# Hand-over from a dense block to routed experts: another place for tile 0's output, a later third routing, other row buffers and eight fact buffers

## The chip, the cores and the metric

The kernel runs on one core of one Trainium2 chip. The metric is the time of one execution on the device in microseconds (us), from the first to the last instruction with what lies around them. A profiled execution gives a trace beside its time. The engines are named as in the profile: PE multiplies matrices, PEld loads PE's weights, ACT (ScalarE) and DVE (VectorE) work element by element, POOL (GpSimd) does small operations and issues indirect DMAs, and SP (SyncE) issues the other DMAs; SPq is SP's queue of them.

## The reference, cut to what matters

```python
x = attention(q, k, v, alpha)            # 3072 tokens of 384
h = x @ w_in; x = (h * sigmoid(h)) @ w_out   # dense block, 384 -> 2048 -> 384
logits = normed(x) @ normed(expert_emb).T / tau
e = argmax(logits); gate = softmax(logits)[e]
for each expert e:                       # 8 experts
    out[mask_e] = gate * (relu(x[mask_e] @ w1[e]) @ w2[e])   # 384 -> 1024 -> 384
```

## The kernel before, in words

Tokens go through in blocks of 384, eight in all. The attention of later chunks runs among the dense products of earlier blocks. After a block, `route` is called three times, once for 128 tokens: it squares the row for its norm (L1199), takes the logits and the best expert (L1201 to L1212), counts each token's place in its expert with two small matmuls (L1216, L1217, into `pr`), puts the row in two half-precision words (L1234, L1235), works out its position (L1245) and scatters it with an indirect DMA on POOL (L1248) into `xs_d`, a list in DRAM sorted by expert. A row of 394 words is 384 of data and 10 of facts (token, scale, logits).

After that the expert tiles run, 128 rows of the list each. Tile j has these steps:

- `prep_load(j)`: SP loads the tile's data with a transposing DMA into `xT` (L1440) and its facts into `mt` (L1441). Eight early tiles (0 to 7) have a list of their own, `idx0`, made before the last block ends. For the others `tile_list` makes `idx` on DVE (L1332 to L1399), in words of `g3`, after the last routing.
- `expert1(j, 0)` and `expert1(j, 1)`: 9 matmuls each (L1495) into `hp2`, relu into two half-precision parts on ACT (L1501) and DVE (L1502), in the scratch tile `work`. `send(j, i)` lets SP turn that half with a transposing DMA (L1468): halves of even tiles into `hb` and into `g3[:, 0:1024]`, those of odd tiles into `work`.
- `expert2(j)`: 24 matmuls (L1523) into `po`, the first 12 from the first turned half and the others from the second; ACT scales `po` into `ob` (L1531) and POOL scatters `ob` to the output (L1534).

The last block's three routings (`last(0)`, `last(1)`, `last(2)`) are written among the steps of tiles 0 to 3. POOL also writes rows of padding behind each expert's list, eight DMAs from DRAM to DRAM (L1409). Up to shortly before the hand-over, SP also loads the experts' second weights in pieces (L736); ACT and DVE, or ACT and POOL, split each piece into two half-precision words (L691 and L692, or L560, L563 and L564). The last of these pieces share ACT and DVE with tile 0's relu.

Three things set the order around the change. Each engine and each queue takes its instructions in the order that the built program gives it. This order comes from a scheduler, which goes by the order of the code and its own reckoning. A tile of a pool with `bufs=3` takes one of three places, and waits until its reader before has ended. The row pool (tag "row", three buffers, below A, B and C) holds `xT`, the rows of `route`, and before the change tile 0's `ob`. Tag "sq" is one further buffer; `last(0)`'s row and the later `ob` take turns in it. Before the change buffer A holds tile 0's `xT`, then `last(1)`'s row, then tile 4's `xT`; B holds tile 1's `xT`, tile 0's `ob`, then `last(2)`'s row; C holds the `xT` of tiles 2, 3 and 5.

Of the kernel before, what the change touches and what calls it, by code (L numbers as in the profile page):

```python
# [9 lines left out]
FP32 = mybir.dt.float32  # L10
# [263 lines left out]
def attention_silu_moe_kernel(  # L274
# [57 lines left out]
    NT, DM = out.shape  # L332
# [19 lines left out]
    ROW = DM + E + 2  # L352
# [12 lines left out]
    def guard(kind, thr=0.0, op=ALU.is_lt):  # L365
        if kind not in guards:
            width = {"decay": 2 * NCH, "nat": NCH, "finite": 160}.get(kind, 8)
            t = const.tile([128, width], FP32, name=f"guard_{kind}")
            nc.vector.memset(t, 2.0 * thr if op == ALU.is_lt else 0.0)
            guards[kind] = [t, 0, thr, op]  # L370
        g = guards[kind]
        g[1] += 1
        return g[0][:, g[1] - 1:g[1]]
# [39 lines left out]
    if True:  # L413
# [4 lines left out]
        m2 = wst.enter_context(tc.tile_pool(name="m2", bufs=2, side="right"))  # L418
# [12 lines left out]
        def bank(dims, dtype, name):  # L431
            at = (ps_a, "at")
            wide = [at, at, at, (ps_o, "o0"), (ps_o, "o1"), (ps_o, "o2"), (ps_h, "h"), (ps_h, "h")]
            pool, tag = at if turn[0] is None else wide[turn[0] % 8]
            if turn[0] is not None:
                turn[0] += 1
            return pool.tile(dims, dtype, tag=tag, name=name)
# [12 lines left out]
        g3 = m2.tile([128, 4 * BLK], FP16, name="g3", bufs=1)  # L450
# [966 lines left out]
        def parts(j):  # L1417
            if j < KEARLY:
                return [(slice(0, 128), idx0[0:1, j:j + 1], ei0[0:1, j:j + 1])]
            if j < NFULL:  # L1420
                n = j - KEARLY
                return [(slice(0, 128), idx[0:1, n:n + 1], ei[0:1, n:n + 1])]
            cols = [2 * (j - NFULL) + h for h in range(2)]
            return [
                (slice(64 * h, 64 * h + 64), idx[0:1, NLIST + e:NLIST + e + 1], e) for h, e in enumerate(cols)
            ]

        def prep_load(j):
            d = tl_[j] = {"s": (j - NFULL + SFULL if j >= NFULL else j) % 2}
            d["x"] = xT = m2.tile([128, 2 * KD, 128], FP16, tag="row", name="xT", bufs=3)  # L1430
            mt = m2.tile([128, ROW - DM], FP32, tag="mt", name="mt", bufs=6)
            loads = []
            for ts, src, _ in parts(j):
                r = nc.values_load(
                    src, engines=sp, min_val=0, max_val=DUMMY,
                    skip_runtime_bounds_check_because="a tile starts inside an expert's rows or at the dummy rows",
                )
                size = ts.stop - ts.start
                loads += [
                    nc.sync.dma_start_transpose(out=xT[:, :, ts], in_=xs_d.bitcast(FP16)[bass.ds(r, size), 0:2 * DM]),  # L1440
                    nc.sync.dma_start(out=mt[ts], in_=xs_d[bass.ds(r, size), DM:]),  # L1441
                ]
            if j < KEARLY:
                for ins in loads:
                    for other in scattered[NCH - TPB:] + pads:
                        tc.declare_no_dep(ins.ins, other.ins, reason="early tiles hold tokens of earlier blocks only")
                early_loads.extend(loads)
            d["m"] = mt
# [17 lines left out]
        def send(j, i):  # L1466
            d = tl_[j]
            lead["send"] = nc.sync.dma_start_transpose(  # L1468
                out=d["hT"][i].rearrange("p (c t) -> p c t", t=128), in_=d["hs"][i].rearrange("p s f -> p (s f)")
            )  # L1470

        def expert1(j, i, keep=False):
            d = tl_[j]
            if i == 0:
                d["e"] = [
                    (ts, src if isinstance(src, int) else nc.values_load(
                        src, engines=[mybir.EngineType.PE], min_val=0, max_val=E - 1,
                        skip_runtime_bounds_check_because="the chip clamps the index to an expert",
                    )) for ts, _, src in parts(j)
                ]  # L1480
                s = d["s"]
                d["hs"] = [
                    work[:, 512 * at:512 * (at + 1)].bitcast(FP16).rearrange("p (s f) -> p s f", s=2)
                    for at in ((3, 2) if s else (5, 4))
                ]
                odd = work[:, 0:1024].bitcast(FP16)
                d["hT"] = (odd[:, 0:1024], odd[:, 1024:2048]) if s else (hb, g3[:, 0:1024])
            xT = d["x"]
            fs = slice(i * 512, (i + 1) * 512)
            hp = ps_h.tile([128, 512], FP32, tag="h", name="hp2")  # L1490
            n = 0
            for c in range(KD):
                for a, w in ((c, "h"), (KD + c, "h"), (c, "l")):
                    for ts, e in d["e"]:
                        nc.tensor.matmul(  # L1495
                            out=hp[ts], lhsT=xT[:, a, ts], rhs=w1s[w][c][:, e if isinstance(e, int) else bass.ds(e, 1), fs],
                            start=(n == 0), stop=(n == 3 * KD - 1),
                        )
                    n += 1
            hs = d["hs"][i]  # L1500
            lead["a"] = nc.scalar.activation(out=hs[:, 0], in_=hp, func=ACTF.Relu)  # L1501
            lead["g"] = nc.vector.scalar_tensor_tensor(  # L1502
                out=hs[:, 1], in0=hp, scalar=0.0, in1=hs[:, 0], op0=ALU.max, op1=ALU.subtract
            )
            if not keep:
                send(j, i)

        def expert2(j, part=None):
            d = tl_[j] if part == 0 else tl_.pop(j)
            hT = d["hT"]  # L1510
            if part != 1:
                d["o"] = (
                    bank([128, 512], FP32, "po") if j < 2 else ps_o.tile([128, 512], FP32, tag=f"o{d['s']}", name="po")
                )[:, 0:DM]
            po = d["o"]
            order = [[0, 1, 2, 3], [4, 5, 6, 7]] if part is None else [[[0, 1, 2, 3], [4, 6]], [[5, 7]]][part]
            n, total = (3 * 6 if part == 1 else 0), 3 * KE
            for group in order:
                for a, w in ((0, "h"), (0, "l"), (4, "h")):
                    for c in group:  # L1520
                        at = (a + c % 4) * 128
                        for ts, e in d["e"]:
                            nc.tensor.matmul(  # L1523
                                out=po[ts], lhsT=hT[c // 4][:, at + ts.start:at + ts.stop],
                                rhs=w2s[w][c][:, e if isinstance(e, int) else bass.ds(e, 1), :], start=(n == 0), stop=(n == total - 1),
                            )
                        n += 1
            if part == 0:
                return
            ob = m2.tile([128, ROW], FP32, name="ob", **(dict(tag="sq", bufs=1) if j else dict(tag="row", bufs=3)))[:, 0:DM]  # L1530
            nc.scalar.activation(  # L1531
                out=ob, in_=po, func=ACTF.Copy, scale=d["fac"], accum_out=guard("finite", 0.0, ALU.not_equal)
            )
            lead["o"] = nc.gpsimd.indirect_dma_start(  # L1534
                out=out[:, :], out_offset=bass.IndirectOffsetOnAxis(ap=d["row"], axis=0),
                in_=ob, in_offset=None, bounds_check=NT - 1, oob_is_err=False,
            )
# [26 lines left out]
        def block(j):  # L1564
# [3 lines left out]
            if last:  # L1568
                early()
                prep_load(0)  # L1570
                prep_load(1)
                prep_load(2)
# [45 lines left out]
        last = lambda t: route(NCH - TPB + t, acc[t])  # L1618
# [14 lines left out]
        expert1(1, 1)  # L1633
        assert not todo and not late
        expert2(0, 0)
        last(0)
        last(1)
        expert1(2, 0, True)
        expert1(2, 1, True)
        expert2(0, 1)  # L1640
        send(2, 0)
        send(2, 1)
        prep_load(3)
        last(2)
        expert2(1)
        expert1(3, 0)
        expert1(3, 1)
        prep_load(4)
        tile_list()
        order = [*range(SFULL), *range(NFULL, NFULL + SPAIR)]  # L1650
        for n in range(2, len(order)):
            j = order[n]
# [68 lines left out]
```

## Time and profile before

| | us |
|---|---|
| median of three runs | 779.56 (778.83 to 782.80) |
| the profiled execution's own time | 775.31 |
| its span, first to last instruction | 773.7 |
| PE busy in the span | 735.0 (95%) |
| DVE, ACT, POOL busy | 499.1, 414.4, 235.7 |
| mean granted TensorE clock | 0.988 of full |

A busy share is a mean over stages with different limits: the attention and dense stages up to about 535 us, the hand-over from 535 to 580 us, the expert tiles from there. A row of the timeline reads: start, duration, engine, line, operation, what it writes and reads, and in brackets how long the engine had been idle and what ended that. For SPq and POOL DMA rows the duration is that of issuing; when the data lands is not in it.

### The profile page before, as it was taken

The page shows a single profiled execution, that of the slowest core. Times are in us where ns is not written, and L with a number is a line of the kernel's source. Part 1 is how long each engine was busy: PE and PEld are TensorE (multiplying, and loading weights), DVE is VectorE, ACT ScalarE, POOL GpSimd, SP SyncE. Part 2 cuts the span into 40 slices and gives each one's busy share as a digit, 9 for nine tenths or more (in the row PEclk, how much of TensorE's full clock was granted, in tenths as well). Part 3 has the DMA queues.
Part 4 walks back from the last instruction along what each step waited for, and adds up shares of the span by engine and source line. Part 5 has one row for each costly group of instructions (what it writes and reads, how often), then busy time and mean ns, then how long its engine had stood idle before and what let it go on. Part 6 is the DMA issues. An engine that isn't in the chain of part 4 may idle for free. (4 is left out here: it accounts for less than half of the span.)

```text
span 773.7 us, 16578 instructions
## 1 busy us (share of the span) xinstructions
PE 735.0 (95%) x5577; PEld 459.5 (59%) x5577; DVE 499.1 (64%) x1434; ACT 414.4 (54%) x936; POOL 235.7 (30%) x328
## 2 busy tenths in 40 slices
PE   8878989999999999999999999999959999999995
PEld 6746655666676667666666655555425555555553
DVE  7999878677897978887877684766632222121221
ACT  4655556567576766856767675767412222222221
POOL 3404235434453653543243020402222111111111
PEclk9999999999999999999999999999989999999998
DMA  9998453435465555464422464267687666756661
GB/s 208 229 318 224 85 91 56 108 65 100 110 127 134 109 130 116 93 151 93 89 88 71 152 189 142 63 177 237 111 165 142 118 128 122 123 103 120 119 107 40
DMA packets 248204, 99.64 MB, mean 129 GB/s; under 512 B 229145, under 2 KB 237502, under 8 KB 247984
## 3 DMA queue, kind: packets, MB, share of 16 engines
q1 hardware_dynamic: 244528, 87.29, 52.5%
q0 software_dynamic: 3584, 11.18, 4.2%
q8 instruction: 51, 0.84, 0.5%
q14 instruction: 41, 0.34, 0.1%
HBM read 58.39 MB, written 12.16 MB: 91 GB/s over the span
## 5 line engine op out<-in xcount | busy, mean ns | idle before, releaser
L1171 PE MATMUL o<-wo_h,w2l 128*128 128x392 f16 x528 | 145.7, 330 | 2.3 <-DVE w2l L1157 1.7
L1502 DVE SCALAR_TENSOR_TENSOR work<-hp,work 128x512 f16<-128x512 f32 x56 | 38.7, 690 | 145.4 <-ACT work L1501 145.4
L1148 PE MATMUL hp<-w2l,wi_h 128*128 128x384 f16 x480 | 118.7, 326 | 0.3 <-ACT w2l L1155 0.3
L1495 PE MATMUL hp<-w1h,xT 128*128 (+1 forms) x384 | 101.1, 382 | 8.3 <-DMA xT<-xs_d 8.1
L1171 PEld LDWEIGHTS <-w2l 128*128 128x128 f16 x792 | 75.3, 98 | 52.9 <-DVE w2l L1157 4.1
L1148 PEld LDWEIGHTS <-wi_h 128*128 128x128 f16 x768 | 74.6, 98 | 49.6 <-issue 3.0
L1495 PEld LDWEIGHTS <-xT 128*128 128x128 f16 (+1 forms) x576 | 50.5, 101 | 65.5 <-DMA xT<-xs_d 7.9
L1171 PE MATMUL o<-wo_l,w2l 128*128 128x392 f16 x264 | 87.4, 331 | 0.0
L1534 POOL DMA_INDIRECT out_dram<-ob,mt x28 | 27.8, 994 | 175.3 <-ACT ob L1531 167.0
L1148 PE MATMUL hp<-w2l,wi_l 128*128 128x384 f16 x240 | 78.2, 326 | 0.0
L1148 PE MATMUL hp<-w2h,wi_h 128*128 128x384 f16 x288 | 71.4, 329 | 1.4 <-ACT w2l L1155 1.0
L1501 ACT ACTIVATE work<-hp 128x512 f16<-128x512 f32 x56 | 33.3, 596 | 72.7 <-PE hp L1495 71.6
L1157 DVE SCALAR_TENSOR_TENSOR w2l<-w2l 128x384 f16<-128x384 f32 x88 | 54.1, 617 | 22.7 <-ACT w2l L1156 22.5
L1171 PE MATMUL o<-wo_h,g 128*128 128x392 f16 x240 | 67.1, 331 | 1.0 <-DVE g L1157 0.7
L1155 ACT ACTIVATE w2l<-hp 128x384 f32<-128x384 f32 x88 | 42.6, 486 | 40.5 <-PE hp L1148 37.8
L1495 PE MATMUL hp<-w1l,xT 128*128 (+1 forms) x192 | 64.3, 382 | 0.0
L1531 ACT ACTIVATE ob<-po,s 128x384 f32<-128x384 f32 x28 | 16.3, 582 | 82.2 <-PE po L1523 75.9
L895 POOL TENSOR_SCALAR_AFFINE_SELECT S<-S 128x512 f32<-128x512 f32 x48 | 32.9, 710 | 85.4 <-ACT S L894 85.3
L1148 PEld LDWEIGHTS <-wi_l 128*128 128x128 f16 x384 | 37.5, 98 | 26.8 <-DVE wi_l L602 2.6
L1171 PEld LDWEIGHTS <-g 128*128 128x128 f16 x360 | 34.9, 99 | 24.6 <-issue 1.3
L1148 PE MATMUL hp<-w2h,wi_l 128*128 128x384 f16 x144 | 46.2, 326 | 1.7 <-DVE wi_l L602 1.7
L1156 ACT ACTIVATE w2l<-w2l 128x384 f16<-128x384 f32 x88 | 45.7, 524 | 2.3 <-PE o L1171 0.4
(299 smaller groups left out, 1546.6 us busy)
## 6 DMA issues: line engine op xcount, KB each, us to landing
work<-in_moe_w_dram SPq DMA_DIRECT2D x24, 512.0 KB, 3.6
work<-in_moe_w_dram SPq DMA_DIRECT2D x30, 384.0 KB, 3.5
nat_a<-in_alpha_dram SPq DMA_DIRECT2D x23, 192.0 KB, 3.2
nat_k<-in_k_dram SPq DMA_DIRECT2D x23, 192.0 KB, 3.1
nat_q<-in_q_dram SPq DMA_DIRECT2D x23, 192.0 KB, 3.2
nat_v<-in_v_dram SPq DMA_DIRECT2D x23, 192.0 KB, 3.0
w1h<-in_moe_w_in_dram SPq DMA_DIRECT2D x5, 768.0 KB, 6.1
w1h<-in_moe_w_out_dram SPq DMA_DIRECT2D x5, 768.0 KB, 7.5
```

Of the source, the lines that this page charges most:

```text
L895: nc.gpsimd.affine_select(out=s, in_=s, pattern=[[0, NPAIR], [1, 128]], compare_op=ALU.is_ge, fill=0.0, base=0, channel_multiplier=-1,)
L1148: ins = nc.tensor.matmul(out=hp, lhsT=wi[a][f // 2][:, c, (f % 2) * 128:(f % 2 + 1) * 128], rhs=x[:, c, :], start=(n == 0), stop=(n == 3 * ...
L1155: nc.scalar.activation(out=g, in_=hp, func=ACTF.Silu, scale=1.0 / (SX * SWI))
L1156: lead["a"] = nc.scalar.activation(out=gh, in_=g, func=ACTF.Copy, scale=SG)
L1157: lead["g"] = nc.vector.scalar_tensor_tensor(out=gl, in0=g, scalar=SG, in1=gh, op0=ALU.mult, op1=ALU.subtract)
L1171: nc.tensor.matmul(out=acc[t], lhsT=a[:, ts], rhs=wo[w][f // 2][:, f % 2, :], start=(f == 0 and n == 0), stop=(f == KF - 1 and n == 2),)
L1495: nc.tensor.matmul(out=hp[ts], lhsT=xT[:, a, ts], rhs=w1s[w][c][:, e if isinstance(e, int) else bass.ds(e, 1), fs], start=(n == 0), stop=( ...
L1501: lead["a"] = nc.scalar.activation(out=hs[:, 0], in_=hp, func=ACTF.Relu)
L1502: lead["g"] = nc.vector.scalar_tensor_tensor(out=hs[:, 1], in0=hp, scalar=0.0, in1=hs[:, 0], op0=ALU.max, op1=ALU.subtract)
L1531: nc.scalar.activation(out=ob, in_=po, func=ACTF.Copy, scale=d["fac"], accum_out=guard("finite", 0.0, ALU.not_equal))
L1534: lead["o"] = nc.gpsimd.indirect_dma_start(out=out[:, :], out_offset=bass.IndirectOffsetOnAxis(ap=d["row"], axis=0), in_=ob, in_offset=Non ...
```

## The change

Tile 0's `ob` goes into the last 768 half-precision words of `g3`, read as 384 words of 32 bits. Of these the first 256 lie in tile 0's second turned half, which its 24 matmuls have read by then. The loads of tiles 3 and 4 are written before tile 2's second half is sent, and `last(2)` after tile 3's two halves. There are eight `mt` buffers in place of six.

```diff
         def prep_load(j):
             d = tl_[j] = {"s": (j - NFULL + SFULL if j >= NFULL else j) % 2}
             d["x"] = xT = m2.tile([128, 2 * KD, 128], FP16, tag="row", name="xT", bufs=3)
-            mt = m2.tile([128, ROW - DM], FP32, tag="mt", name="mt", bufs=6)
+            mt = m2.tile([128, ROW - DM], FP32, tag="mt", name="mt", bufs=8)
...
-            ob = m2.tile([128, ROW], FP32, name="ob", **(dict(tag="sq", bufs=1) if j else dict(tag="row", bufs=3)))[:, 0:DM]
+            ob = m2.tile([128, ROW], FP32, tag="sq", name="ob", bufs=1)[:, 0:DM] if j else g3[:, 2 * DM:].bitcast(FP32)
...
         expert2(0, 1)
         send(2, 0)
+        prep_load(3)
+        prep_load(4)
         send(2, 1)
-        prep_load(3)
-        last(2)
         expert2(1)
         expert1(3, 0)
         expert1(3, 1)
-        prep_load(4)
+        last(2)
         tile_list()
```

By the addresses in the built program, buffer B now holds tile 1's `xT`, then tile 3's, then `last(2)`'s row; C holds tile 2's `xT`, then tile 4's, then tile 6's; A holds tile 0's, then `last(1)`'s row, then tile 5's `xT`.

The scheduler moves more than the code does. On SP, among the last pieces of the experts' weights, three loads of facts (of tiles 3, 4 and 5) stood before and there are now five. The first two of them have not moved; this is the place of the third, before the change:

```order
L736 DMA work_109<-in_moe2_w2_dram 128x2x384
L1434 TENSOR_LOAD idx0_209
L1441 ISA
L1441 DMA mt_7766<-xs_d_60 128x10
L736 DMA work_109<-in_moe2_w2_dram 128x2x384 x5
```

and with it (the last three rows of facts are those of tiles 5, 6 and 7):

```order
L736 DMA work_109<-in_moe2_w2_dram 128x2x384
L1434 TENSOR_LOAD idx0_209
L1441 ISA
L1441 DMA mt_7765<-xs_d_60 128x10
L1434 TENSOR_LOAD idx0_209
L1441 ISA
L1441 DMA mt_7816<-xs_d_60 128x10
L1434 TENSOR_LOAD idx0_209
L1441 ISA
L1441 DMA mt_7896<-xs_d_60 128x10
L736 DMA work_109<-in_moe2_w2_dram 128x2x384 x5
```

The facts of tiles 6 and 7 stood behind the hand-over's transposes before; now two more reads of the list and two more loads stand ahead of the next five pieces of weights.

Further on, SP at the hand-over, before (`g3` and `hb` are halves of even tiles, `work` from `work` of odd ones; xT_7615, 7716 and 7765 are tiles 3, 4 and 5):

```order
L1468 DMA_TRANSPOSE g3_179<-work_109 128x8x128
L1468 DMA_TRANSPOSE work_109<-work_109 128x8x128 x2
L1468 DMA_TRANSPOSE hb_7404<-work_109 128x8x128
...
L1440 DMA_TRANSPOSE xT_7615<-xs_d_60 128x6x128
...
L1441 DMA mt_7817<-xs_d_60 128x10
L1468 DMA_TRANSPOSE g3_179<-work_109 128x8x128
...
L1441 DMA mt_7897<-xs_d_60 128x10
...
L1440 DMA_TRANSPOSE xT_7716<-xs_d_60 128x6x128
L1468 DMA_TRANSPOSE work_109<-work_109 128x8x128 x2
...
L1440 DMA_TRANSPOSE xT_7765<-xs_d_60 128x6x128
```

and with the change (tiles 3, 4 and 5 are xT_7613, 7620 and 7764):

```order
L1468 DMA_TRANSPOSE g3_179<-work_109 128x8x128
L1468 DMA_TRANSPOSE work_109<-work_109 128x8x128
...
L1440 DMA_TRANSPOSE xT_7613<-xs_d_60 128x6x128
L1468 DMA_TRANSPOSE work_109<-work_109 128x8x128
L1468 DMA_TRANSPOSE hb_7404<-work_109 128x8x128
...
L1440 DMA_TRANSPOSE xT_7620<-xs_d_60 128x6x128
L1468 DMA_TRANSPOSE g3_179<-work_109 128x8x128
L1468 DMA_TRANSPOSE work_109<-work_109 128x8x128
...
L1440 DMA_TRANSPOSE xT_7764<-xs_d_60 128x6x128
L1468 DMA_TRANSPOSE work_109<-work_109 128x8x128
L1468 DMA_TRANSPOSE hb_7404<-work_109 128x8x128
```

Tile 3's data moved ahead of tile 1's second turned half, tile 4's into the place that tile 3's had, and tile 5's ahead of tile 3's second turned half. Tile 2's second turned half (the second `g3`) now waits itself for the landing of tile 0's output; before, the facts ahead of it on the queue waited for that. In the built program tile 5's `xT` waits for the landing of `last(1)`'s scatter, as tile 4's did before.

PE behind tile 2's second half (hp2_7590), before:

```order
L1495 MATMUL hp2_7590<-w1l2_6147,xT_6961 128x512
L1216 LDWEIGHTS tri_72
L1216 MATMUL pr_7518<-oh_7516,tri_72 128x8
L1217 LDWEIGHTS ones16_61
L1217 MATMUL pr_7518<-cnt1_85,ones16_61 128x8
L1523 LDWEIGHTS work_109
...
L1523 MATMUL po_7657<-w2h0_6145,work_109 128x384
```

and with the change (hp2_7661 is tile 3's first half):

```order
L1495 MATMUL hp2_7590<-w1l2_6147,xT_6961 128x512
L1495 LDWEIGHTS xT_7613
...
L1495 MATMUL hp2_7661<-w1h0_90,xT_7613 128x512
...
L1216 LDWEIGHTS tri_72
L1216 MATMUL pr_7518<-oh_7516,tri_72 128x8
L1217 LDWEIGHTS ones16_61
L1217 MATMUL pr_7518<-cnt1_85,ones16_61 128x8
...
L1523 MATMUL po_7628<-w2h0_6145,work_109 128x384
```

Tile 3's first half now stands between tile 2's second half and the matmul that counts `last(0)`'s tokens; its second half follows tile 1's products. On POOL the copy of tokens for `last(2)` (L1204), which stood between tile 0's output and `last(0)`'s scatter, follows tile 1's output, and the first four padding DMAs stand in a row where there were two and two with tile 2's output between.

## Rows read from the trace of the kernel before

**Rows 1.** Timeline of PE at the hand-over and in the first tiles behind it

```profile
551.02 0.17 PE L1216 MATMUL pr<-oh,tri 128*128 128x8 f16 x1 [1.39 <-DVE oh L1212]
...
562.46 0.81 PE L1523 MATMUL po<-w2h,g 128*128 x4
571.41 1.01 PE L1495 MATMUL hp<-w1h,xT 128*128 x2 [8.13 <-DMA xT<-xs_d]
...
576.68 0.81 PE L1523 MATMUL po<-w2h,work 128*128 x4
...
580.58 0.59 PE L1495 MATMUL hp<-w1h,xT 128*128 x2
...
584.47 0.81 PE L1523 MATMUL po<-w2h,hb 128*128 x4
```

**Rows 2.** Stretches: busy time of PE, PEld, DVE, ACT, POOL; PEclk; DMA share; GB/s

```profile
572.00:574.00 2.00, 2.00 (x6) 0.69 (x5) 0.00 (x0) 0.00 (x0) 0.00 (x0) 0.50 0.83 207
...
600.00:640.00 40.00, 40.00 (x217) 21.13 (x216) 9.20 (x26) 11.01 (x33) 4.90 (x5) 1.00 0.65 123
```

**Rows 3.** Timeline of SP, POOL and ACT at the hand-over

```profile
543.85 4.88 SPq L1468 DMA_TRANSPOSE work<-work  x2
...
550.97 1.23 SPq L1440 DMA_TRANSPOSE xT<-xs_d  x1
551.03 1.08 POOL L1534 DMA_INDIRECT out_dram<-ob,mt  x1 [0.58 <-issue]
...
555.06 0.37 SPq L1441 DMA_DIRECT2D mt<-xs_d  x1
...
556.10 0.98 POOL L1248 DMA_INDIRECT xs_d<-row,pos  x1 [0.66 <-DVE lg L1201]
...
559.42 0.58 ACT L1531 ACTIVATE ob<-po,s 128x384 f32<-128x384 f32 x1 [0.79 <-DMA xs_d<-row,pos]
...
561.75 0.97 POOL L1248 DMA_INDIRECT xs_d<-row,pos  x1 [0.30 <-DVE cn L1334]
...
564.64 1.24 SPq L1440 DMA_TRANSPOSE xT<-xs_d  x1
```

**Rows 4.** DMA view: issues, count, KB each, median us to landing

```profile
work<-in_moe_w_dram SPq DMA_DIRECT2D x30, 384.0 KB, 3.5
...
xT<-xs_d SPq DMA_TRANSPOSE x32, 3.2
work<-work SPq DMA_TRANSPOSE x28, 3.5
...
mt<-xs_d SPq DMA_DIRECT2D x24, 5.0 KB, 1.8
...
g<-work SPq DMA_TRANSPOSE x14, 4.6
```

**Rows 5.** Timeline of SP from 518 to 524 us

```profile
520.18 0.39 SPq L736 DMA_DIRECT2D work<-in_moe_w_dram  x1
521.08 0.33 SPq L1441 DMA_DIRECT2D mt<-xs_d  x1
521.51 2.34 SPq L736 DMA_DIRECT2D work<-in_moe_w_dram  x3
```

**Rows 6.** Timeline: last weight pieces, tile 0's turned half, PE behind it

```profile
525.76 0.84 ACT L691 ACTIVATE w2h<-work 128x768 f16<-128x768 f32 x1 [0.46 <-DMA work<-in_moe_w_dram]
...
527.42 1.68 POOL L564 TENSOR_TENSOR w2l<-work,w2h 128x768 f16<-128x768 f32 x1 [18.65 <-ACT w2h L563]
...
532.93 0.84 ACT L691 ACTIVATE w2h<-work 128x768 f16<-128x768 f32 x1 [0.79 <-DMA work<-in_moe_w_dram]
...
535.92 1.27 SPq L1468 DMA_TRANSPOSE hb<-work  x1
...
539.15 0.81 PE L1523 MATMUL po<-w2h,hb 128*128 x4 [0.93 <-DMA hb<-work]
```

**Rows 7.** Tile `work`, 560 to 600 us: issue to landing of its transposes

```profile
DMA to landing us min/median/max: 3.1/3.8/7.8
```

## The prediction

> **What bounds the kernel now.** I read the stretches first: from 600 to 640 us PE is busy 40.00 of 40 us at a clock of 1.00 [rows 2], so behind the hand-over the expert tiles are bound by PE, and whatever the hand-over saves or loses arrives whole at the end. Then PE's timeline at the hand-over, for its brackets. PE stands still for 1.39 us before the matmul that counts the first routing's tokens, and for 8.13 us before tile 4's first matmul, for its data [rows 1]. Behind the long wait the clock is 0.50, the lower level, 1.2 GHz [rows 2]: tile 4's two halves take from 571.41 to 576.68, 5.27 us, and tile 5's at the upper level from 580.58 to 584.47, 3.89 us [rows 1]. So 1.38 us more go to the clock. Then the queues, for who made tile 4 wait. Its `xT` was issued at 564.64, on SP, behind a scatter issued on POOL at 561.75 [rows 3], because its row buffer held that scatter's row. That scatter had been late since 551.03, when POOL put out tile 0's output and, behind it, waited for its landing to copy tokens into the same buffer; the first routing's scatter went out only at 556.10 [rows 3].
>
> **What the change removes.** All three: 1.39 + 8.13 + 1.38 = 10.9 us.
>
> The 1.39: PE does tile 3's first half there instead. A tile's two halves take 3.89, so one takes 1.95; PE comes to the counting matmul 1.95 - 1.39 = 0.56 us after its mask is ready. Tile 3's data has to be there at 551.02 - 1.39 = 549.63. On SP it now stands between the two transposes that began at 543.85 and took 4.88 together [rows 3]; one issue of a transpose takes 1.23 to 1.27 [rows 3, 6], so SP was idle for some 2.4 between them. Issued at 545.1, with 3.2 to landing [rows 4], it is there at 548.3.
>
> The 8.13: tile 4's `xT` takes the place of tile 3's old one, issued at 550.97 [rows 3], and lands by 554.2. PE needs it after tile 3's first half, tile 1's products (3.90, from 576.68 to 580.58 [rows 1]), tile 3's second half and tile 2's products: 549.6 + 1.95 + 3.90 + 1.95 + 3.90 = 561.3. It has 7 us to spare.
>
> The 1.38: without a long wait I see no reason for the clock to fall; the 1.39 wait of before left no row at the lower level.
>
> **What stands in its place, wait by wait.** Tile 2's second turned half goes to SP once tile 0's output has landed, as now seen in the facts that waited for it at 555.06 [rows 3]. With 4.6 to landing, the median for `g` [rows 4], it is there at 559.7; PE wants it after tile 1's products, tile 3's second half and the first 12 matmuls of tile 2: 549.6 + 1.95 + 3.90 + 1.95 + 1.95 = 559.4. That is a wait of 0.3. Behind it on SP are tile 3's first turned half, tile 5's data and tile 3's second turned half. Tile 5's data now waits for the second routing's scatter. POOL is free of the copy between, so the first scatter goes out when its position is known, by my estimate about 554 (PE now counts its tokens at 551.6, and on DVE tile 2's relu stands ahead of the position), and the second about 556, after the counting matmul within tile 1's products. A scatter lands 3.3 after its issue (556.10 to 559.42 [rows 3]): 559.3. Tile 5's issue takes 1.24, and tile 3's second half, issued at 560.6 with 3.5 to landing [rows 4], is there at 564.1. PE wants it at 561.6 + 3.89 + 1.95 = 567.4. 3.3 us to spare.
>
> The ACT work for `ob` of tile 0 is the same instruction with another address: nothing. The third routing and the tile list go behind tile 3's products; DVE and POOL do them under PE's work on tiles 2 to 4, and their result is first used by tile 8, two PE tiles after the padding. That hides them; without that cover they would cost up to the 10.7 us that separate tile 0's output at 551.03 from the second scatter at 561.75 [rows 3].
>
> **What it adds.** The two fact loads on SP ahead of five weight pieces. One such load with its read of the list takes SP from 520.57 (end of the piece at 520.18) to 521.51: 0.94 [rows 5]. Two are 1.88: the piece issued at 521.51 goes out at 523.4. Is that covered? ACT waited 0.46 for it at 525.76 [rows 6]; it landed 4.2 after its issue. From there I find a chain without slack: ACT splits it, then another piece whose low half POOL makes at 527.42 to 529.10; this frees the scratch words for a further piece, for which ACT waits again (0.79 at 532.93). Behind that piece on ACT and DVE stands tile 0's relu, then SP's turning of it at 535.92, then PE's wait of 0.93 at 539.15 [rows 6]. So a slip at 521 lengthens that 0.93. Everything at the hand-over then shifts by the same amount, so that the sums above hold. Bounds: 1.88 if the piece again needs 4.2; 1.1 if it needs the median of 3.5 [rows 4], since its neighbours on the queue have drained. I take 1.5, between ends that are close; 0 is excluded, since 523.4 + 3.5 is already later than 525.76.
>
> Of that last addition the Trainium skill has a harsher view: in "DMA: Bandwidth & Descriptors", section "Rules for kernel authors", it says to coalesce small transfers, since "under 64 KB you're paying mostly overhead", and these are 5 KB each. Under "Anatomy of one DMA", it gives a fixed cost of about 2.0 us per DMA; two would be 4.0 (an estimate by that page), and the sum by it 10.9 - 4.0 - 0.3 = 6.6. The row speaks for less: SP goes on to the next load in 0.94, before any landing.
>
> **The sum.** -10.9 + 1.5 + 0.3 = -9.1 us. The profiled execution took 775.31 (span 773.7), so it would take 766.2. That execution lies 4.25 below the median of the runs, 779.56, and the runs themselves spread over 4 us. I take the same 9.1 from the median: **770.5 us**. Its own range, by the bounds (1.1 to 1.88 for the loads, 0 to 1.5 for the wait for `g`), is a gain of 7.5 to 9.8, 769.8 to 772.1. A change of under 0.5%, 3.9 us, is about what a measurement of this kernel can't tell from none.
>
> **Rivals.**
> 1. The fact loads cost nothing that PE sees (the weight pieces catch up). For it: PE itself waits for nothing of theirs until 539.15, 18 us after the slip. Against: the waits of 0.46, 0.79 and 0.93 in one line [rows 6]. Gain 10.6, 769.0 us. Chance 0.14.
> 2. The fact loads hold the queue until they land. 1.8 to landing [rows 4] in place of 0.94 gives 3.6 for two. Against it: 521.08 to 521.51 [rows 5]. Gain 10.9 - 3.6 - 0.3 = 7.0, 772.6 us. The Trainium skill's fixed cost per DMA ("DMA: Bandwidth & Descriptors") points the same way. Chance 0.09.
> 3. The gain is given back one tile later. Four padding DMAs in a row, where two and two stood, go out behind the third routing, whose counting matmul now stands inside tile 4's second half, which ends at 561.6 + 3.89 = 565.5; with position and scatter, about 567.5. Just then SP turns tile 4's second half, behind its relu and tile 6's data. Among two and two a transpose took up to 7.8 to land [rows 7]; if four take twice that, 15.6, tile 4's half issued at 567.6 lands at 583.2. PE wants it at 561.6 + 3.89 + 3.90 + 3.89 + 1.95 = 575.2. A wait of 8, and 1.4 for the clock: a gain of -0.3, 779.9 us, no change. PE waits from a landing time of 7.6 on, and the gain falls under 3.9 from about 11.4 (a wait of 3.8, and 1.4 for the clock). Chance 0.07.
> 4. Slower: tile 5's data, waiting on SP for the second routing's scatter, blocks tile 3's second turned half behind it. With 3.3 us to spare, PE stops when the scatter lands after 562.6. To be slower by 3.9, it must land 9.1 + 3.9 - 1.4 = 11.6 later still, at 574, 18 us after its issue, where 3.3 was read: 783.5 us and up. A POOL queue whose scatters wait for one another would do it. Chance 0.03.
>
> That the change does nothing is out: the buffers have other holders and PE another order.
>
> **Chances.** Forecast 0.67. Faster by over 0.5%: forecast, rivals 1 and 2, 0.90, less 0.02 for spread between runs: 0.88. Within 0.5%: rival 3 and that 0.02, 0.09. Slower: 0.03. The range that holds the forecast and rivals 1 and 2, with 2 us on either side for the spread of the runs (3.2 above and 0.7 below their median): 767 to 774.5.
>
> **What would show it.** The waits of 1.39 and 8.13 are gone from PE, and no stretch between 540 and 600 shows a clock below 1.00. PE's wait for `hb` grows from 0.93 to about 2.4, which shows the fact loads' price; if it stays at 0.93, rival 1 holds; at 3 or more, rival 2. A new row `po` waiting for `g` is at most 1.5. The first routing's scatter goes out about 2 us earlier than 556.10, plus the shift. Tile 5's first matmul stands about 9 us before 580.58. Wrong would be: a wait of PE of over 4 us anywhere from 555 to 590 (rivals 3, 4), or a gain of the hand-over that does not arrive at the end.

## The result, and the profile after

The changed kernel took 770.34 us (median of six runs, 766.58 to 773.80), the kernel before 779.19 on the same chip (six runs). The ratio is 0.9886, 95% interval 0.9847 to 0.9925: a gain of 8.9 us, where 9.1 was forecast. The profiled execution took 770.93, its span is 769.3.

PE's timeline at the hand-over and behind it, changed kernel, beside [rows 1] and the last of [rows 6]:

```profile
541.72 0.81 PE L1523 MATMUL po<-w2h,hb 128*128 x4 [1.33 <-DMA hb<-work]
...
554.01 0.17 PE L1216 MATMUL pr<-oh,tri 128*128 128x8 f16 x1
...
562.60 0.81 PE L1523 MATMUL po<-w2h,g 128*128 x4 [0.52 <-DMA g<-work]
...
564.59 0.59 PE L1495 MATMUL hp<-w1h,xT 128*128 x2
...
572.45 0.59 PE L1495 MATMUL hp<-w1h,xT 128*128 x2
...
580.23 0.59 PE L1495 MATMUL hp<-w1h,xT 128*128 x2
...
600.71 0.81 PE L1523 MATMUL po<-w2h,work 128*128 x4 [0.86 <-ACT ex L1456]
...
603.19 0.81 PE L1523 MATMUL po<-w2h,work 128*128 x4 [0.37 <-DMA work<-work]
...
635.32 0.81 PE L1523 MATMUL po<-w2h,work 128*128 x4 [0.82 <-DMA work<-work]
```

The counting matmul (554.01) and tile 4's first (564.59) have no bracket any more: the waits of 1.39 and 8.13 are gone. Tile 5 begins at 572.45, tile 6 at 580.23. New are small waits in tile 7's two groups of products (600.71, 603.19). The first names ACT; the same matmul in the next execution waits for the turned half (below), which I take for its releaser here too. A third, of 0.82, stands at tile 11's second half (635.32); I have not followed what made that half late.

Stretches of the same execution, columns as in [rows 2]:

```profile
570.00:580.00 10.00, 10.00 (x58) 5.48 (x56) 5.59 (x30) 2.05 (x6) 4.65 (x8) 1.00 1.11 211
...
600.00:640.00 40.00, 37.97 (x204) 19.98 (x205) 8.42 (x24) 9.85 (x30) 4.86 (x5) 1.00 0.64 118
```

The clock stays at its upper level through the hand-over. But from 600 to 640 PE is busy for 37.97 us, where it was 40.00 in [rows 2]: the three waits named (0.86, 0.37, 0.82).

SP, changed kernel:

```profile
522.34 0.39 SPq L736 DMA_DIRECT2D work<-in_moe_w_dram  x1
523.24 2.00 SPq L1441 DMA_DIRECT2D mt<-xs_d  x3
525.34 6.87 SPq L736 DMA_DIRECT2D work<-in_moe_w_dram  x5
...
553.42 1.24 SPq L1440 DMA_TRANSPOSE xT<-xs_d  x1
...
564.05 1.22 SPq L1440 DMA_TRANSPOSE xT<-xs_d  x1
565.36 1.26 SPq L1468 DMA_TRANSPOSE work<-work  x1
...
592.62 4.07 SPq L1441 DMA_DIRECT2D mt<-xs_d  x5
596.79 1.26 SPq L1468 DMA_TRANSPOSE work<-work  x1
```

The second routing's scatter on POOL, for which tile 5's data (564.05 above) waits on SP:

```profile
558.94 0.97 POOL L1248 DMA_INDIRECT xs_d<-row,pos  x1 [1.25 <-DVE pos L1245]
```

The three loads of 523.24 stand where one stood in [rows 5]. Tile 4's data goes out at 553.42, in [rows 3] at 564.64. And five fact loads in a row, 4.07 us, stand ahead of tile 7's first turned half at 596.79. The kernel before has three there; its SP:

```profile
599.73 2.29 SPq L1441 DMA_DIRECT2D mt<-xs_d  x3
602.12 1.25 SPq L1468 DMA_TRANSPOSE work<-work  x1
```

To compare executions I use three marks on PE: tile 0's products (541.72 above), tile 6's first matmul (580.23), and the guards' matmul (L1680) at the end. Before, the first is in [rows 6], and the others are these:

```profile
588.37 0.59 PE L1495 MATMUL hp<-w1h,xT 128*128 x2
...
765.95 0.17 PE L1680 MATMUL pb<-bad,ones 128*128 128x10 f16 x1 [1.58 <-DVE bad L1547]
```

In the changed kernel the last is at 761.32. So the span's -4.4 (773.7 to 769.3) is made up so: up to the first mark +2.57, first to second 49.22 to 38.51, -10.71; second to third 177.58 to 181.09, +3.51; behind it +0.23. Of the +2.57, 2.16 had already arisen ahead of the added fact loads (weight piece at 522.34, at 520.18 in [rows 5]); the profiled execution of before was among the quicker ones up to there (the third of the thirteen below to reach the first mark).

### The profile page after: what moved, and what is told of

Same layout as the page of the kernel before. It is cut to its first block, busy times and chain, and to the rows that moved or that the text cites. A ratio compares the mean times of both kernels' runs of the same rounds, so it can differ in the third digit from the quotient of the medians.

```text
span 769.3 us, 16571 instructions
## 1 busy us (share of the span) xinstructions
PE 736.4 (96%) x5577; PEld 460.2 (60%) x5577; DVE 499.4 (65%) x1434; ACT 414.0 (54%) x936; POOL 235.7 (31%) x328
## 5 line engine op out<-in xcount | busy, mean ns | idle before, releaser
L1523 PEld LDWEIGHTS <-work 128*128 128x128 f16 (+1 forms) x384 | 33.3, 101 | 24.8 <-DMA work<-work 3.2
```

The lines of the kernel that those rows point to most:

```text
L1523: nc.tensor.matmul(out=po[ts], lhsT=hT[c // 4][:, at + ts.start:at + ts.stop], rhs=w2s[w][c][:, e if isinstance(e, int) else bass.ds(e, 1) ...
```

## The experiments

The middle columns come from the three marks in each profile, one execution of each kernel; "loads" is the count of fact loads in a row on SP ahead of tile 7's first turned half, the last column PE's waits in tile 7's products. Kernels with one letter share a chip and its runs of before (medians 779.19 on A, 780.62 on B, 781.73 on C, 781.11 on D).

| kernel | chip | median us | ratio to before, 95% | mark 1 to 2 | mark 2 to 3 | loads | wait, tile 7 |
|---|---|---|---|---|---|---|---|
| before | A | 779.19 | 1 | 49.22 | 177.58 | 3 | 0 |
| changed | A | 770.34 | 0.9886 (0.9847 to 0.9925) | 38.51 | 181.09 | 5 | 1.23 |
| 1 changed, again | B | 772.54 | 0.9874 (0.9833 to 0.9915) | 38.37 | 182.04 | 5 | 1.98 |
| 2 six fact buffers | B | 768.91 | 0.9841 (0.9793 to 0.9889) | 38.90 | 179.25 | 3 | 0.26 |
| 3 place only | B | 774.84 | 0.9908 (0.9878 to 0.9937) | 41.84 | 180.52 | 3 | 0 |
| 4 sequence only | B | 774.02 | 0.9900 (0.9863 to 0.9938) | 41.55 | 179.57 | 3 | 0 |
| 5 seven fact buffers | C | 771.59 | 0.9855 (0.9817 to 0.9894) | 38.70 | 181.62 | 4 | 1.91 |
| 6 before, eight | C | 779.88 | 0.9981 (0.9956 to 1.0007) | 51.14 | 178.92 | 5 | 0.98 |
| 7 facts spread | C | 767.17 | 0.9806 (0.9768 to 0.9843) | 38.11 | 178.98 | 1 | 0 |
| 8 place, tile 5 later | C | 774.65 | 0.9900 (0.9864 to 0.9936) | 41.83 | 178.50 | 3 | 0 |
| 9 place, tiles 5, 6 later | D | 770.32 | 0.9860 (0.9830 to 0.9890) | 38.35 | 178.15 | 3 | 0 |
| 10 loads behind halves | D | 764.31 | 0.9785 (0.9755 to 0.9816) | 38.15 | 177.30 | 1 | 0 |
| 11 facts spread, again | D | 767.33 | 0.9834 (0.9804 to 0.9864) | 38.43 | 178.30 | 1 | 0 |

My theory after the result: the hand-over gave what was forecast, and the fact buffers, priced at the wrong place, took part of it back near 600. The rivals: that stall belongs to one execution, or to the paddings.

### The changed kernel again

> The changed kernel once more, beside the others. Theory (the hand-over gives 10.7 us back and something new behind it takes about 2): about 770.3 us, PE again stands for 0.5 to 1 us, two or three times, between 598 and 606 us, in tile 7's products and next to them. Rival (that stall was of one execution only): PE is busy for 40.00 of 40 us from 600 to 640, and the time is nearer 768.

PE behind tile 6's start:

```profile
595.98 0.81 PE L1523 MATMUL po<-w2h,g 128*128 x4 [1.19 <-DMA g<-work]
603.65 0.81 PE L1523 MATMUL po<-w2h,work 128*128 x4 [1.60 <-DMA work<-work]
606.14 0.81 PE L1523 MATMUL po<-w2h,work 128*128 x4 [0.38 <-DMA work<-work]
```

The stall at tile 7 is back, larger, so it isn't of one execution. Another stands before it, at tile 6's second half (1.19), which I had not named.

### Six fact buffers

```diff
-            mt = m2.tile([128, ROW - DM], FP32, tag="mt", name="mt", bufs=8)
+            mt = m2.tile([128, ROW - DM], FP32, tag="mt", name="mt", bufs=6)
```

> The changed kernel with six fact buffers as before. In the built program SP has three fact loads in a row ahead of the last weight pieces in place of five, and three ahead of tile 7's first turned half in place of five; tile 6's load stands just ahead of tile 2's second turned half. Theory (the two extra loads ahead of tile 7's half are what PE waits for at 600): no wait of PE between 595 and 610, PE's wait for hb back from 1.33 to about 0.9, its wait for g up from 0.5 to about 1.4 since one load (0.9) now stands ahead of it; in all 1.0 to 2.0 us under the changed kernel, some 769. First rival (the stall at 600 has another cause, the paddings or the third routing): the waits at 600 stay, time within 0.5 of the changed kernel. Second rival (the fact buffers are needed, as tile 6's load holds SP for tile 0's output): a wait of PE for g of 3 us or more, time 772 or more.

PE, then SP:

```profile
540.00 0.81 PE L1523 MATMUL po<-w2h,hb 128*128 x4 [0.94 <-DMA hb<-work]
561.28 0.81 PE L1523 MATMUL po<-w2h,g 128*128 x4 [1.50 <-DMA g<-work]
```

```profile
555.75 0.37 SPq L1441 DMA_DIRECT2D mt<-xs_d  x1
...
591.42 2.24 SPq L1441 DMA_DIRECT2D mt<-xs_d  x3
```

All three waits came in the size that the theory gave: 0.94 for `hb`, 1.50 for `g` (tile 6's load at 555.75 goes ahead of it), and 0.26 at tile 7. So the first rival is out, and the second too: six buffers hold nothing up for long. That the load ahead of `g` makes its 1.50 is not shown: kernel 5 has such a load there (552.78) and no wait, kernel 10 has none and waits 0.79. The time, 3.6 under the kernel with eight on the same chip, points the same way; the two intervals overlap.

### The place of tile 0's output alone

Kernel before, with the `ob` line of the change and nothing else.

> The kernel before with only tile 0's output moved into the dead turned half; sequence and six fact buffers as before. By the addresses tile 3's data then follows tile 1's, tile 4's follows tile 3's own, and the third routing's row follows tile 2's data. Theory (the output in the row pool was the cause of both waits): the waits of 1.39 and 8.13 and the low clock are gone; tile 4's data can be issued when tile 3's second half has been multiplied, about 560, and lands about 563.5, just when PE wants it, so PE waits there 0 to 1.5; time 769 to 771.5. Rival (tile 4's row buffer needs the new sequence too): PE waits 3 us or more for tile 4's data, the clock falls to 0.50 behind it, time 774 or more.

PE, then SP:

```profile
565.71 0.59 PE L1495 MATMUL hp<-w1h,xT 128*128 x2 [0.38 <-issue]
...
572.57 0.81 PE L1523 MATMUL po<-w2h,work 128*128 x4 [2.17 <-DMA work<-work]
```

```profile
560.08 5.93 SPq L1440 DMA_TRANSPOSE xT<-xs_d  x2
566.11 1.26 SPq L1468 DMA_TRANSPOSE work<-work  x1
```

The place alone removes both waits and the low clock (1.00 from 572 to 576); tile 4 waits 0.38. The theory missed what comes next: 2.17 for tile 3's second turned half. Of the two transposes that began at 560.08 the second is tile 5's data, which waits for the second routing's scatter and holds that half behind it until 566.11. That is rival 4's mechanism, at a small price. The time, 774.84, is the one forecast for the rival (774 or more) and 3.3 over the theory's range, but the rival's mechanism, a wait of 3 or more for tile 4's data and the low clock, did not come.

### The sequence alone

Kernel before, with the moved lines (`prep_load(3)`, `prep_load(4)`, `last(2)`) and nothing else.

> The kernel before with only the new sequence; tile 0's output stays in the row pool and there are six fact buffers. By the addresses tile 4's data then takes the buffer of tile 0's output, the third routing's row that of the second routing's. Theory (what held tile 4 was the second scatter, and that was late by the copy of tokens into tile 0's output buffer): tile 4's data is issued about 555, when tile 0's output has landed, 8 us before PE wants it; the wait of 8.13 and the low clock are gone, the 1.39 ahead of the counting matmul stays, time 769.5 to 771.5. Rival (without the new place of tile 0's output nothing is won): a wait of 5 us or more for tile 4's data, time 775 or more.

PE, then POOL:

```profile
554.68 0.17 PE L1216 MATMUL pr<-oh,tri 128*128 128x8 f16 x1 [1.39 <-DVE oh L1212]
...
567.51 0.59 PE L1495 MATMUL hp<-w1h,xT 128*128 x2
...
574.19 0.81 PE L1523 MATMUL po<-w2h,work 128*128 x4 [0.61 <-issue]
576.97 0.59 PE L1495 MATMUL hp<-w1h,xT 128*128 x2 [0.66 <-DVE base L1395]
```

```profile
565.73 0.19 POOL L1204 COPY row<-tok 128x1 int32<-128x1 int32 x1 [3.31 <-DMA xs_d<-row,pos]
```

The 8.13 goes here as well (567.51 is tile 4), the 1.39 stays, as forecast. The copy of tokens still waits for a landing (3.31, now for the second scatter), but behind both scatters, where tile 4's data doesn't need it. So either part alone takes the long wait away: mark 1 to 2 falls by 7.4 and 7.7, together by 10.7. They aren't a sum, since both cut the same chain. The time, 774.02, missed both forecasts: it is 2.5 over the theory's range and 1 under the rival's.

Of the sequence only one thing counts for SP, POOL and the row buffers, by the built programs: with `last(2)` back between tile 2's sends and tile 1's products, or `prep_load(4)` back behind tile 3's halves, SP and POOL still get the same order and the row buffers the same holders, as long as `prep_load(4)` stands ahead of `last(2)` in the code. Then tile 4's `xT` asks for a row buffer before the third routing does. With `last(2)` put back so, PE, ACT and DVE have another order in places; no run shows the time of these two programs.

### Seven fact buffers, and eight in the kernel before

> The changed kernel with seven fact buffers: four fact loads in a row ahead of tile 7's first turned half, where eight buffers give five and six give three. Theory (each load there holds the turned half back by some 0.9): PE's wait in tile 7's products, near 600, lies between that of six (0.26) and of eight (1.23 and 1.98 in two executions), 0.5 to 1.2 in all; its wait for g stays at about 1.5, since tile 7's load now stands ahead of it in place of tile 6's. Time between 769 and 771.5. Rival (the wait near 600 has nothing to do with the loads): it is as large as with eight, 1.2 or more, or nothing.

PE, then SP:

```profile
598.81 0.81 PE L1523 MATMUL po<-w2h,work 128*128 x4 [1.60 <-DMA work<-work]
601.23 0.81 PE L1523 MATMUL po<-w2h,work 128*128 x4 [0.31 <-DMA work<-work]
```

```profile
591.65 3.16 SPq L1441 DMA_DIRECT2D mt<-xs_d  x4
```

> The kernel before with eight fact buffers and nothing else. Theory: the two loads ahead of the weight pieces lengthen PE's wait for hb from 0.93 to 1.1 to 1.4; the waits of 1.39 and 8.13 stay, though tile 6's and 7's loads no longer stand on the queue among the hand-over's transposes; five loads in a row ahead of tile 7's first turned half make PE wait 1 to 2 near 605; in all 0.5 to 2.5 us slower than the kernel before. Rival (they take something off the hand-over): the 8.13 falls by 1 or more, and the time is at or under that of before.

PE, then SP, kernel before with eight:

```profile
575.86 1.01 PE L1495 MATMUL hp<-w1h,xT 128*128 x2 [9.08 <-issue]
616.36 0.81 PE L1523 MATMUL po<-w2h,work 128*128 x4 [0.98 <-DMA work<-work]
```

```profile
605.83 4.08 SPq L1441 DMA_DIRECT2D mt<-xs_d  x5
```

Both partly missed. With four loads the stall is 1.91, as large as with five: it isn't graded by 0.9 a load. And no wait for `g` showed in that execution, where 1.5 was expected. With eight in the kernel before, the stall is there (0.98), the long wait isn't shortened (9.08), but the time doesn't show the price: 779.88 against 781.73, interval from 3.4 us faster to 0.5 slower. What the profiles bear out is the yes or no: with four or five loads in a row all four executions wait 0.98 to 1.98 at tile 7, with three or fewer all nine wait 0 to 0.26.

### The fact loads spread

```diff
-            mt = m2.tile([128, ROW - DM], FP32, tag="mt", name="mt", bufs=8)
+            mt = m2.tile([128, ROW - DM], FP32, tag="mt", name="mt", bufs=6)
...
-            d["m"] = mt
+            d["m"] = mt; j > 4 and behind(loads[-1], lead["send"])
```

> The changed kernel with six fact buffers, and from tile 5 on each tile's fact load behind the turned half that is sent last before it in the code, so that no more than two stand together on SP. Theory (loads in a row, and the one ahead of tile 2's second turned half, cost what they hold back): PE's wait for hb 0.9 to 1.1, for g back to about 0.5, none near 600; about 1 us under the kernel with six buffers, 767.5 to 768.5. Rival (the wait for g comes of tile 0's output landing late, and not of the load): it stays at 1.5, and the time is that of six buffers.

> The kernel with spread facts once more, beside the one with all loads behind the halves, on the same chip: some 767 us, one wait of PE near 594 (1.16 in the execution before) that varies with the landing of the last padding, 0 to 1.6; none for the fact loads.

PE, then SP, first execution:

```profile
561.47 0.87 PE L1523 MATMUL po<-w2h,g 128*128 x4 [0.24 <-DMA g<-work]
...
594.26 0.87 PE L1523 MATMUL po<-w2h,g 128*128 x4 [1.16 <-DMA g<-work]
```

```profile
587.04 1.23 SPq L1440 DMA_TRANSPOSE xT<-xs_d  x1
588.53 0.35 SPq L1441 DMA_DIRECT2D mt<-xs_d  x1
588.98 2.55 SPq L1468 DMA_TRANSPOSE g<-work  x1
```

The wait for `g` is back to 0.24 (0.45 in the second execution), none stands at tile 7, and the time is 767.2 and 767.3. What is left is the wait at tile 6's second half, 1.16 and 0.83. Ahead of that half on SP stands tile 8's data (587.04), which in the built program waits for the landing of the last padding, issued by 583.58; SP's waits show 2.0 us for such a landing there.

### The place alone, with tile 5's data later, then tile 6's too

Kernel 3 with one line more:

```diff
-            d["m"] = mt
+            d["m"] = mt; j == 5 and behind(loads[0], lead["send"])
```

> The kernel before with only tile 0's output in the dead half, and on SP tile 5's data behind tile 3's second turned half instead of ahead of it; nothing else moves on any engine. Theory (with the place alone PE waited 2.17 for tile 3's second turned half because tile 5's data stood ahead of it on SP and waited for the second routing's scatter): that wait is gone or under 0.7, first products of tile 0 to first matmul of tile 5 falls from 33.2 to 31.0 to 31.7, time 1.5 to 2 us under the place alone. Rival (the turned half itself is slow to land, beside the padding): the wait stays at about 2.

PE, then SP:

```profile
577.40 0.81 PE L1523 MATMUL po<-w2h,hb 128*128 x4 [1.39 <-DMA hb<-work]
581.06 0.81 PE L1523 MATMUL po<-w2h,g 128*128 x4 [1.55 <-DMA g<-work]
```

```profile
570.49 1.28 SPq L1440 DMA_TRANSPOSE xT<-xs_d  x1
571.87 1.26 SPq L1468 DMA_TRANSPOSE hb<-work  x1
```

The 2.17 went, as the theory said, and nothing was gained: 1.39 and 1.55 came in its place (mark 1 to 2 is 41.83, before this 41.84). Tile 6's data, at 570.49, now is the first on SP to wait for a scatter, the third, and tile 4's halves stand behind it. Putting tile 6's `prep_load` behind tile 4's halves in the code tests that:

> The kernel before with tile 0's output in the dead half, and on SP tile 5's data behind tile 3's second turned half (as in the run before) and tile 6's behind tile 4's second turned half. Theory (in the run before, the 2.17 went, and 1.39 and 1.55 came in its place, because tile 6's data, now first to wait for a scatter, the third, stood ahead of tile 4's turned halves): both waits are gone or under 0.5 each; first products of tile 0 to first matmul of tile 6 falls from 41.83 to 39.0 to 39.8 (38.5 in the changed kernel), time 2 to 3 us under that run, near 771.5. Rival (tile 4's halves land late because the four paddings run at that time): waits of 1 us or more stay at tile 4's products.

PE at the second mark, its largest wait since the first:

```profile
578.97 0.59 PE L1495 MATMUL hp<-w1h,xT 128*128 x2 [0.30 <-issue]
```

Mark 1 to 2 fell to 38.35, no wait is over 0.30 between these marks, and the time to 770.32. So with the place alone and two loads put later the whole gain is had without the new sequence.

### All late loads behind the halves

```diff
-            mt = m2.tile([128, ROW - DM], FP32, tag="mt", name="mt", bufs=8)
+            mt = m2.tile([128, ROW - DM], FP32, tag="mt", name="mt", bufs=6)
...
-            d["m"] = mt
+            d["m"] = mt; j > 4 and [behind(i, lead["send"]) for i in loads]
...
-            if n + 3 < len(order):
-                prep_load(order[n + 3])
             if 2 < n and n + 1 < len(order):
                 expert1(order[n + 1], 0)
                 expert1(order[n + 1], 1)
+            if n + 3 < len(order):
+                prep_load(order[n + 3])
```

> The changed kernel with six fact buffers and, from tile 5 on, each tile's data and facts behind both turned halves that PE wants sooner. Theory (what PE still waits for behind the hand-over, 0.3 to 1.6 us at a time, are turned halves behind a load on SP, above all tile 6's behind tile 8's data, which waits for the last padding): no wait of PE between 570 and 755 over 0.3; 1 to 1.5 us under the kernel with spread facts, some 766. Rival (these halves land late by themselves): waits of 0.3 to 1.2 remain in two or three places, time within 0.5 of the kernel with spread facts.

PE's waits from 562 us to the end, then a stretch:

```profile
PE pb L1680 <- DVE bad L1547: 1.6, 1, 1.6
```

```profile
600.00:640.00 40.00, 40.00 (x219) 21.23 (x217) 9.49 (x27) 10.28 (x30) 4.88 (x5) 1.00 0.64 118
```

Behind 562 us no wait is left but that of the guards' matmul. The median is 764.31: 6.0 under the changed kernel's own 770.34 by medians of two chips, and by ratios 0.9785 against 0.9886 and 0.9874. Against the spread facts on the same chip it is 3.0 faster by the medians, twice what I expected; the intervals overlap a little. The two profiled executions have one span, 762.5, as that of the spread facts was its quickest. From the first mark to the third they differ by 1.28 (215.45 against 216.73), of which 0.83 is the wait at tile 6's half that the theory named. Behind the third mark 6.27 us remain, 7.24 in the spread kernel and 7.98 in the changed one; I have not followed that.

## Why the prediction was right, and where its steps were off

- **The hand-over** (10.9 less 0.3 for `g`, that is 10.6): 10.71 and 10.85 between the first two marks in two executions, both against the one profile of before (49.22; with eight fact buffers alone it was 51.14). Waits, clock and the wait for `g` (0.52 and 0.40) came as worked out.
- **Tile 5's data** had "3.3 us to spare" ahead of tile 3's second half. It went out at 564.05, where 559.3 was reckoned, 561.9 with the shift of 2.57 at the first mark. The scatter was not late: it was issued at 558.94, 556.4 without the shift, and 556 was reckoned. But SP went on only 5.1 after its issue, having waited 3.7 for its landing (SP's waits from 556 to 566 us), where 3.3 was read from one scatter of before. PE didn't wait, but the place alone showed how near it was (2.17).
- **The fact loads among the weight pieces** (1.5) were oversized. The slip on SP was there: the five pieces began 3.00 after the piece ahead of them (522.34 to 525.34), 1.33 before (520.18 to 521.51 in [rows 5]), so 1.67. But from that piece to tile 0's products it is 19.38, 20.31 and 20.77 with five early loads, and 18.97 to 19.99 in the six kernels with three: 0.4 more in the first pair of profiles, 0.7 by the means. PE's wait for `hb` was 1.33, 1.15 and 1.15 with five, and 0.93, 0.94, 1.36, 0.94, 1.02 and 1.15 with three; in some kernels of either kind PE also waits 0.7 to 1.0 for DVE shortly ahead of it. By the prediction's own sign (about 2.4 for the forecast, 0.93 for rival 1) that is nearer to rival 1, which had a chance of 0.14. The failed step is "a chain without slack": SP waits among those five pieces for scratch words anyway. From the piece at 522.34 to the end of their issue it is 9.87 us in the changed kernel, 10.21 and 10.03 in the two others with five, and 9.14 to 10.28 with three.
- **Rival 2** (the loads hold the queue until they land) is out: five loads took SP 4.07, 0.81 each, and not the 1.8 that one takes to land. The fixed cost that the Trainium skill gives ("DMA: Bandwidth & Descriptors", "Anatomy of one DMA"), about 2.0 us for each DMA, is given there for DMAs issued by GpSimd, and the section puts most of it down to completion. It is near the landing of these loads, which SP issues (1.8 in [rows 4]); as a price on SP, two loads for 4.0, it did not hold.
- **What was missed** is the other place where eight buffers move loads: ahead of tile 7's first turned half, 1.23 and 1.98 of waiting. I had read only the first place at which the order changes. Its price and what the 1.5 was too large by nearly cancel: that the sum came out right to 0.2 us is luck, though the large term, the hand-over, is not. The spread of the runs, 7 us, would not have told a miss of 1.
- **The eight buffers** thus bring nothing: with six the hand-over is as short to 0.5 us. Their cost at tile 7 is shown by the profiles' waits, 1.5 in the mean of the four kernels with four or five loads. Between the second and third mark the means of these four and of the six with three are 180.9 and 178.9, but single kernels overlap (178.92 with five, 180.52 with three), since other waits fall there too; the times alone don't separate it.
- **Rival 3** (four paddings in a row) is out: no wait at tile 4's products in the changed kernel. A later padding does delay tile 8's data and through it tile 6's half, by 0 to 1.2 us.

## What to carry to other kernels

When a queue has one order, a load that must wait for something late belongs behind every transfer that is wanted sooner, even if its own buffer is free; here that, with six fact buffers, was worth some 6 us beyond the change, 1.7 of them behind the third mark, where I have not followed them. When a buffer count is raised, look at every place where the scheduler pulls loads forward, above all at the end of what gated them: they come out together, ahead of whatever was next. And two cures of one chain don't add up: try each alone before crediting both.

## What the runs showed of the hardware

- A wait of 2.17 us (place alone) left the granted clock at 1.00 behind it; the waits of 8.13 and 9.08 left rows at 0.50 and 0.54 (576 to 581 us, kernel before with eight buffers).
- The time at which tile 0's products start varied from 538.31 to 543.20 us between the thirteen profiles, by more than most edits here moved anything; in the two kernels that were profiled twice the time from the first mark to the second agrees to 0.14 and 0.32 us, from the second to the third to 0.95 and 0.68.
- From the end of the last paddings' issue to tile 8's data going out it took 2.5 us in the changed kernel's first execution (584.37 to 586.85) and 3.8 in the next (585.90 to 589.66), with copies of the same size.
